# Sixteen small moves inside the core against one store to memory and four loads back, with a new order of the whole kernel

## The chip, the cores and the metric

The kernel runs on 1 core of a Trainium2 chip. The metric is the device time of one execution in microseconds (us), as the median of the runs; before, three runs took 598.32 to 598.87 us, the median 598.42 us. The engines are PE (TensorE: matmul, with PEld for its weight loads), DVE (VectorE), ACT (ScalarE), POOL (GpSimd) and SP (SyncE, which here only issues transfers). SBUF is the core's working memory, PSUM the memory that PE writes, DRAM the memory outside the core.

## The reference

Eight batches of 512 tokens in 8 heads of 64, and 32 states in each head, attend to each other; then everything goes through one feed-forward layer:

```python
scores = scale * np.matmul(x, state.transpose(0, 1, 3, 2))      # tokens read the states
a = softmax(scores); xread = np.matmul(a, state)
scores2 = scale * np.matmul(state, x.transpose(0, 1, 3, 2))     # states read the tokens
a2 = softmax(scores2); sread = np.matmul(a2, x)
y = concatenate([xread, sread], axis=2)                         # (8, 8, 544, 64) -> 4352 rows of 512
h = y @ w_in                                                    # 512 -> 2048
out = (h * clip(h + 3, 0, 6) / 6) @ w_out                       # 2048 -> 512
```

The inputs are x (8, 8, 512, 64), state (8, 8, 32, 64), w_in (512, 2048) and w_out (2048, 512), all float32; the output is (4352, 512).

## The kernel before, in words

**Steps.** The feed-forward layer is cut into 144 steps: 16 for each of the 8 batches of tokens, and 16 for the rows of all states together at the end. A step has a first product (`first`, `first_grouped`, `first_states`; lines 1225 to 1419 and 1664) into one of two PSUM banks `ps_h`. ACT and DVE then make g = h * clip(h + 3, 0, 6) of it (lines 1413 and 1416 in batches 0 to 2, lines 1250, 1252 and 1261 in batches 3 to 7, where seven blocks take the place of eight), and split g into a high and a low half of fewer bits (lines 460 to 497). In many steps of the later batches the low half is finished by a transfer of POOL that accumulates (line 497, 128 x 896 elements or so). The second product (`second`, `second_grouped`) multiplies the halves with those of w_out and adds up in four banks `acc0` to `acc3`. Every product is three matmuls on halves (line 1178). The tokens' own reading of the states is folded into the weights: `wprime` (line 768) multiplies the states with w_in (matmuls of line 700), and the first product takes the softmax weights `aT` against that.

**The attention of batch b** is spread over earlier steps. The states come in through four small transfers on SP's queue (`load_state`, line 634) and DVE transposes them (`turn_state`, line 645). x comes in twice, once as it is (`load_x`, line 668, tile `xb`, four quarters) and once in blocks for a transposition by DVE (`load_turned`, line 686, sixteen transfers into tiles `raw`; `take_in`, line 846). PE makes the scores (line 700, in `scores_by_columns`). DVE and ACT make the two softmaxes; `states` (line 1006) writes the exponentials of the states' scores into tiles `tmp`, key `e2` (ACT, line 1041). Batch 0 has a way of its own at the start of the kernel: PE transposes x (line 857), ACT copies it (line 864), PE makes the scores (line 921), and DVE takes the maximum (line 934) and so on.

**Around the change.** `weights_moved(b)` (line 1088, batches 1 to 7) turns the exponentials of one batch, 128 x 1024 float32, so that PE can use them as weights. DVE transposes blocks of 32 x 32 (line 1096) from `e2` into a tile `raw`, key `blocks`. Then sixteen transfers on SP's queue (line 1103) move the quarters of the partitions across: quarter q of `blocks`, part c, goes to partitions of quarter c, part q, of another `raw` tile, key `e2T`. One transfer is 32 partitions by 256 elements, 32 KB, from SBUF to SBUF. The reader is `tokens_read(b)` (line 1117): 64 small matmuls (line 1134) of `e2T` with x, which ride with the scores of batch b + 1 in one task of PE (`riders`, lines 971 to 989); batch 7's stand alone (line 1155).

**Tiles and order.** `raw` has three places (five from batch 2 on) that weights, turned x, `blocks` and `e2T` use in turn. Each piece of work is told to a `Plan` (line 192) with its engine, an assumed cost, what it reads and writes. The order in which all of it is issued, on every engine and queue, is one long list of numbers, `ORDER` (line 68, 2986 numbers); the plan only checks that it keeps the dependencies, and finds places for the tiles. Each engine and SP's queue work in that order and wait at the first thing that isn't ready.

Of the kernel before, what the change touches and what calls it, by code (L numbers as in the profile page):

```python
# [68 lines left out]
1 0 5 2 3 4 24 79 92 426 27 34 28 6 30 36 37 11 31 35 29 38 32 43 44 33 39 45 49 40 46 47 41 50 56 25 48 51 42 26 52  # L69
61 57 53 80 58 74 62 130 54 63 77 55 59 81 64 60 75 82 65 68 14 95 76 66 78 67 93 87 71 69 94 72 107 70 88 96 108 90  # L70
109 89 12 97 73 114 154 7 91 110 13 429 102 111 132 19 115 103 113 112 105 104 116 127 8 427 117 126 85 106 83 120 131
161 171 9 144 84 118 133 121 10 15 134 145 119 138 128 16 137 86 135 129 136 122 153 17 166 123 100 18 151 169 101 152
167 124 139 168 150 170 98 125 188 146 99 430 147 195 20 205 183 148 206 21 196 157 207 149 189 193 158 22 194 190 155
217 23 186 156 178 184 191 187 212 223 164 210 192 222 159 214 431 224 185 225 165 162 160 228 218 174 219 271 141 229
163 215 238 220 204 237 142 221 209 143 235 230 213 239 428 216 245 172 140 211 175 259 247 173 236 262 260 234 263
176 261 233 240 179 290 177 181 241 180 254 246 231 182 281 232 264 272 208 505 276 201 291 244 202 274 338 243 203
288 273 322 287 275 286 242 250 295 279 251 282 289 248 283 298 277 249 296 284 280 297 252 278 285 308 292 255 253
506 299 257 256 307 293 258 265 294 332 267 309 316 337 335 304 333 305 268 317 300 306 266 336 315 269 334 226 301
323 310 339 302 270 311 324 318 314 303 358 312 340 352 368 359 367 319 325 353 364 341 369 365 354 326 313 507 360
327 363 342 361 375 508 403 362 320 343 366 404 321 373 344 405 412 374 370 197 355 399 345 400 328 417 371 346 347  # L80
504 348 372 376 424 349 408 420 402 422 421 411 418 423 394 350 329 425 330 351 401 413 410 395 419 409 509 396 495
331 406 414 397 432 415 398 514 416 437 441 407 513 440 446 356 227 462 433 448 377 465 443 466 439 517 469 379 464
434 392 496 438 198 468 497 199 463 435 383 457 467 498 511 499 470 471 384 357 436 458 389 512 459 478 381 510 479
390 476 460 387 629 477 378 461 445 481 472 525 518 473 487 380 482 486 385 516 488 388 474 489 382 631 475 535 447
483 515 386 501 484 393 536 502 391 485 634 444 500 537 442 503 519 572 635 454 630 452 449 538 542 590 450 579 540
453 573 480 549 539 451 575 543 455 577 576 541 456 632 578 200 551 558 520 636 580 568 521 530 633 570 775 522 552
638 574 544 640 591 550 545 569 644 546 592 523 637 524 547 639 548 563 493 606 526 494 527 587 607 594 564 595 571
608 586 650 565 490 609 589 593 491 553 581 566 612 531 661 528 642 627 567 619 596 532 588 616 582 667 626 597 643
690 669 621 641 583 622 666 670 614 584 668 776 777 662 677 613 585 610 663 685 678 625 533 778 684 534 623 664 700
598 492 529 665 618 779 645 628 708 780 620 707 624 683 679 615 682 599 680 617 709 701 749 681 695 784 611 717 702  # L90
655 705 703 783 706 710 656 600 657 716 559 704 740 805 658 601 711 715 659 741 806 660 714 560 742 748 554 807 602
745 555 796 561 743 556 562 781 603 712 557 713 604 746 754 771 797 605 747 646 772 812 799 744 773 798 801 795 647
802 765 651 800 782 652 671 794 803 774 787 766 804 767 770 788 792 722 768 789 817 723 691 785 769 718 692 719 825
696 693 720 672 823 694 697 673 724 793 790 725 827 674 721 791 698 832 818 699 675 834 828 819 676 826 820 829 824
838 835 821 830 930 822 857 831 733 833 759 727 858 877 839 732 836 837 726 750 867 731 760 887 751 863 859 728 888
786 860 883 730 865 755 884 729 861 653 869 862 648 756 752 900 761 649 878 762 912 654 879 889 885 866 880 868 763
870 882 931 764 910 917 846 881 808 841 906 809 923 753 864 901 925 913 908 918 902 922 757 813 924 919 758 886 814
911 909 1012 920 903 921 847 810 815 734 1005 927 1013 929 735 1004 1015 904 1011 1014 1006 905 848 1009 736 1010 1017
1016 972 842 962 914 849 851 843 1019 928 844 852 999 845 963 1018 895 1020 1008 1000 964 907 811 926 915 1007 1001
965 1041 890 853 1002 854 932 1003 916 966 1042 855 967 737 1043 850 1047 689 935 973 896 1059 840 891 933 946 975 892  # L100
1051 1039 970 936 1069 968 1070 1037 934 1049 937 1064 1071 1060 1048 893 1053 1040 938 894 1067 974 1066 1044 1038
971 1068 969 1065 1086 1057 1045 1076 1061 1046 947 939 1062 856 1052 1094 897 1063 816 1055 940 1058 1100 1050 1082
948 1099 738 1088 1056 949 739 1054 1102 1106 1077 1085 941 1103 898 1084 1072 1078 899 1104 1105 942 1089 1079 1107
1074 1080 1073 1081 1087 1202 1095 1075 1029 1101 1117 687 1115 1032 1096 1090 1119 686 956 1083 1121 1036 943 1097
1026 1092 1113 1028 1098 1132 1033 1091 1126 1108 1130 1034 1203 1116 1035 1118 1109 1120 1205 1133 1129 1093 1030
1128 1110 1134 944 1111 1023 1204 1112 1127 1024 1122 1144 1206 1114 688 1146 1123 1021 1142 957 1161 1124 950 871
1131 1157 1125 1164 1031 1148 1162 1025 1165 1135 1027 958 1158 1163 1140 1022 959 1143 945 1160 1153 1149 1155 1136
1154 1141 1255 993 1137 1166 1138 1256 1150 960 1151 1145 1257 1156 961 1182 1258 1152 1167 1139 1259 1193 1183 1168
1147 1195 1159 1169 1184 1190 1196 1189 1185 1291 1186 1191 1170 1292 1192 976 1178 1171 1194 1207 1293 1187 1172 1177
1180 1188 1173 1208 1181 1174 1200 1209 1175 1176 1197 1179 1210 1239 1199 1211 1296 1212 1260 1240 1213 991 872 1214  # L110
1247 981 994 1261 1250 1217 1241 978 1198 1219 995 987 1252 1294 1242 1248 1251 982 1262 996 1249 1243 983 1254 1253
1218 1297 1221 1244 985 1215 1216 986 1276 1263 990 1245 1295 1246 1285 977 1264 1220 1274 873 1289 984 1287 1277 1222
989 1269 1275 1283 988 1265 1319 980 874 1266 992 997 1333 1267 1331 979 1320 1271 875 1273 1201 1278 1286 876 1227
1279 1335 998 1280 1321 1281 1284 1290 1329 1322 1288 1336 1367 1282 1337 1327 1368 1347 1323 1383 1369 1324 951 1370
1298 1371 1325 1338 1326 1339 1332 1268 953 1312 1381 1334 1377 1300 1343 1379 1313 1299 1314 1301 1375 1270 1315 1330
1348 1302 1349 1328 1340 1272 1231 1345 1344 1233 1303 1372 1394 1223 1346 952 1407 1373 1304 1341 1235 1374 1318 1305
1376 1384 1380 1396 1397 1382 1408 1392 1385 1391 1393 1401 1378 1306 1386 1390 1399 1226 1342 1387 1395 1225 1409
1423 1388 1230 1316 1410 1400 1317 1228 1411 1433 1350 1398 1234 1437 1419 1224 1412 1442 1307 1355 1389 1424 1450
1229 1413 1422 1443 1420 1425 1421 1414 1236 1417 1444 1438 1456 1354 1576 1426 1356 1445 1418 1415 1579 1427 1232
1436 1402 1577 1432 1353 1434 1454 1580 1428 1238 1435 1446 1431 955 1429 1475 1361 1416 1447 1308 1462 1430 1439 1237  # L120
1448 1491 1440 1453 1513 1463 1471 1449 1359 1477 1360 1578 1357 1464 1469 1365 1457 1508 1465 1366 1309 1473 1362
1511 1485 954 1452 1512 1310 1487 1466 1474 1493 1352 1514 1478 1509 1489 1479 1488 1494 1510 1476 1486 1472 1467 1470
1480 1492 1451 1495 1455 1613 1363 1481 1502 1496 1482 1468 1506 1358 1504 1500 1614 1364 1497 1546 1616 1351 1483
1548 1615 1498 1484 1503 1501 1490 1617 1544 1565 1499 1550 1563 1507 1311 1559 1515 1403 1405 1404 1536 1406 1529
1459 1460 1551 1516 1547 1537 1458 1549 1517 1560 1530 1518 1535 1562 1552 1531 1532 1538 1545 1566 1519 1564 1553
1666 1567 1581 1539 1554 1669 1540 1570 1505 1561 1555 1582 1597 1541 1583 1556 1568 1635 1542 1557 1584 1543 1585
1591 1569 1558 1589 1605 1586 1609 1670 1595 1598 1606 1587 1612 1608 1441 1588 1610 1667 1571 1647 1649 1599 1611
1607 1636 1668 1645 1643 1600 1651 1601 1637 1602 1596 1592 1638 1593 1533 1603 1652 1594 1639 1590 1604 1658 1671
# [1792 lines left out]
```

## Time and profile before

| | |
|---|---|
| median of three runs | 598.42 us |
| the profiled execution, its own time | 598.21 us |
| its span, first to last instruction | 596.4 us |
| mean granted clock of PE | 0.999 |
| instructions in the profile | 13389 |
| PE busy | 589.0 us, 99% |
| DVE busy | 481.6 us, 81% |
| ACT busy | 389.3 us, 65% |
| transfers of line 1103 | 112 of 32 KB |

The profile shows one execution. Busy time is the share in which an engine had an instruction under way; PE's matmuls are pipelined, so that their records overlap. Issuing a transfer doesn't count as busy. The chain of waits is followed back from the last instruction, at each step to what released it.

### The profile page before, as it was taken

To read this page: it belongs to the slowest core of one execution; us is meant where nothing else is said; L and a number is where in the kernel's file an instruction comes from. 1 tells how busy PE (TensorE), PEld (TensorE's weight loads), DVE (VectorE), ACT (ScalarE), POOL (GpSimd) and SP (SyncE) were. 2 spreads that over 40 slices of the span, in tenths; PEclk is the share of its full clock that TensorE was granted. 3 is DMA by queue.
4 is the path that set the end of the run, shared out by engine and by line. 5 is a ranking of instruction groups with operands and counts; after the bars stand their busy time and mean duration, and the time that the engine had idled before them with its cause. 6 is when DMAs were issued, how large, how long until landed. Compare 5 with 4: busy or idle time off the path is not lost.

```text
span 596.4 us, 13389 instructions
## 1 busy us (share of the span) xinstructions
PE 589.0 (99%) x5331; PEld 452.9 (76%) x5331; DVE 481.6 (81%) x911; ACT 389.3 (65%) x637; POOL 89.8 (15%) x112
## 2 busy tenths in 40 slices
PE   8999999999999999999999999999999999999997
PEld 6577778778654445888788877887888888888875
DVE  5989896598877998889999988978889977885342
ACT  5889788885868876757474747555646656473432
POOL 2000000113344311311011111111111111001000
PEclk9999999999999999999999999999999999999999
DMA  8999224567898894597553776785343732323002
GB/s 298 334 281 259 68 90 144 100 151 129 114 114 111 165 145 61 84 197 107 94 114 45 129 125 91 117 144 88 73 58 72 129 71 34 67 32 67 2 1 71
DMA packets 101951, 68.24 MB, mean 114 GB/s; under 512 B 67712, under 2 KB 94976, under 8 KB 101504
## 3 DMA queue, kind: packets, MB, share of 16 engines
q0 software_dynamic: 14400, 21.37, 29.5%
q1 hardware_dynamic: 87200, 45.82, 28.3%
q8 instruction: 42, 0.69, 0.5%
q10 hardware_dynamic: 288, 0.20, 0.1%
q14 instruction: 21, 0.17, 0.1%
HBM read 33.41 MB, written 8.91 MB: 71 GB/s over the span
## 4 chain that ended last, share of the span: by engine, by line
PE 93%; DVE 2%; SPq 2%; issue 1%; ACT 1%; DMA 0%; DVEq 0%
PE acc L1178 54%; PE ps_h L1178 30%; PE both L700 5%; PE ps_h L1134 1%; SPq L1103 1%; PE acc L1449 1%; PE ps_h L1890 1%; PE ps_h L700 1%; DMA st_raw<-in_state_dram 0%; SPq L634 0%; PE both L921 0%; SPq L686 0%; DVE w_in L576 0%; ACT g_hi L494 0%; DVE ot L936 0%
## 5 line engine op out<-in xcount | busy, mean ns | idle before, releaser
L1178 PE MATMUL ps_h<-aT,wp 128*128 128x256 f16 (+2 forms) x1146 | 163.6, 291 | 0.0
L1178 PEld LDWEIGHTS <-g_hi 128*128 128x128 f16 x1344 | 130.7, 98 | 34.3 <-issue 2.6
L1178 PE MATMUL acc<-w,g_hi 128*128 128x256 f16 (+1 forms) x704 | 130.8, 297 | 0.0
L1178 PEld LDWEIGHTS <-wp 128*128 128x128 f16 x1056 | 102.6, 98 | 24.6 <-issue 2.8
L1178 PE MATMUL acc<-T,g_hi 128*128 128x256 f16 x640 | 101.4, 273 | 0.7 <-ACT g_hi L494 0.7
L1178 PE MATMUL acc<-w,g_lo 128*128 128x256 f16 (+1 forms) x352 | 84.0, 297 | 0.0
L1178 PEld LDWEIGHTS <-g_lo 128*128 128x128 f16 x672 | 64.9, 98 | 20.3 <-issue 3.8
L1250 ACT ACTIVATE G<-ps_h,three 128x512 f32<-128x512 f32 x54 | 41.9, 777 | 37.9 <-PE ps_h L1178 26.3
L1178 PE MATMUL acc<-T,g_lo 128*128 128x256 f16 x320 | 64.2, 273 | 0.0
L497 POOL DMA_DIRECT2D g_lo<-G x34 | 29.3, 862 | 165.2 <-DVE g_lo L495 82.7
L1261 DVE TENSOR_TENSOR G<-G 128x256 f32<-128x256 f32 (+1 forms) x108 | 52.2, 486 | 1.7
L1178 PE MATMUL acc<-w_out_hi,g_hi 128*128 128x512 f32 x124 | 50.4, 406 | 0.0
L1178 PE MATMUL acc<-w_out_hi,g_lo 128*128 128x512 f32 x124 | 48.4, 390 | 0.0
L1178 PE MATMUL acc<-w_out_lo,g_hi 128*128 128x512 f32 x124 | 48.3, 390 | 0.0
L1413 ACT ACTIVATE g<-ps_h,three 128x512 f32<-128x512 f32 x48 | 34.3, 717 | 16.5 <-PE ps_h L1178 12.3
L1252 DVE SCALAR_TENSOR_TENSOR G<-G,ps_h 128x512 f32<-128x512 f32 x54 | 36.8, 682 | 6.7 <-ACT G L1250 6.6
L494 ACT CAST g_hi<-G 128x896 f16<-128x896 f32 x34 | 31.7, 934 | 14.6 <-DVE G L1261 9.8
L497 POOL DMA_DIRECT2D g_lo<-g x26 | 22.7, 873 | 122.2 <-DVE g_lo L495 72.6
L1416 DVE SCALAR_TENSOR_TENSOR g<-g,ps_h 128x512 f32<-128x512 f32 x48 | 32.5, 681 | 7.4 <-ACT g L1413 7.3
L468 DVE SCALAR_TENSOR_TENSOR g_lo<-G,g_hi 128x896 f16<-128x896 f32 (+1 forms) x31 | 26.3, 851 | 10.9 <-ACT g_hi L467 6.3
L1654 POOL DMA_DIRECT2D w_out_hi<-w_out_lo x16 | 17.4, 1196 | 116.9 <-PE acc L1178 113.9
L467 ACT ACTIVATE g_hi<-G 128x896 f16<-128x896 f32 (+1 forms) x31 | 23.4, 758 | 17.5 <-DVE G L1261 7.4
(200 smaller groups left out, 983.1 us busy)
## 6 DMA issues: line engine op xcount, KB each, us to landing
xb<-in_x_dram SPq DMA_DIRECT2D x32, 256.0 KB, 3.9
g_lo<-G POOLq DMA_DIRECT2D x34, 224.0 KB, 4.2
raw<-in_x_dram SPq DMA_DIRECT2D x112, 64.0 KB, 3.5
out_dram<-ot SPq DMA_DIRECT2D x10, 512.0 KB, 3.6
early<-in_moe_w_in_dram SPq DMA_DIRECT2D x5, 1023.0 KB, 6.6
w_out_hi<-w_out_lo POOLq DMA_DIRECT2D x16, 256.0 KB, 5.4
g_lo<-g POOLq DMA_DIRECT2D x18, 224.0 KB, 4.0
raw<-raw SPq DMA_DIRECT2D x112, 32.0 KB, 2.9
```

The source lines that it names most:

```text
L467: S(cost, rank, lambda: nc.scalar.mul(hi(), src(), by()), [*reads, *keys], first_, after)
L468: V_(cost, rank, lambda: nc.vector.scalar_tensor_tensor(lo(), src(), by(), hi() if hi().dtype == F16 else hi().bitcast(F32), op0=ALU.mult, ...
L494: S(cost, rank, lambda: nc.scalar.copy(hi(), src()), reads, [writes[0]], after)
L497: P__(0.87, rank, lambda: nc.gpsimd.dma_start(lo(), src(), accum_op=ALU.add), reads, [writes[1]], (), size)
L700: nc.tensor.matmul(out[q // 2 if by_pairs else u][at * NS : (at + 1) * NS, :], (made["stT", b] if left is None else left)[rows, cols], mov ...
L1178: nc.tensor.matmul(ps, l, r, start=start and k == 0, stop=stop and k == len(pairs) - 1)
L1250: S_(0.73, rank, lambda: nc.scalar.activation(g(), h(), AF.Relu, bias=three_of(G_SCALE / 4), scale=scales["gate7"]()), [ps, ("scale", "gat ...
L1252: V(0.63, rank, lambda: nc.vector.scalar_tensor_tensor(g(), g(), 6.0 * G_SCALE / 4, h(), op0=ALU.min, op1=ALU.mult), [ps], [key])
L1261: V(cost, rank, lambda out=out, one=one, other=other, op=op: nc.vector.tensor_tensor(blocks(*out), blocks(*one), blocks(*other), op=op), [ ...
L1413: S_(cost + (0.12 if scaled else 0.05), rank, lambda: nc.scalar.activation(g(), bank(ps)[:, :width], AF.Relu, bias=three_of(by), scale=sca ...
L1416: V(cost, rank, lambda: nc.vector.scalar_tensor_tensor(g(), g(), 6.0 * by, bank(ps)[:, :width], op0=ALU.min, op1=ALU.mult), [ps], [g_key])
L1654: X("P", 0.87, rank, lambda w=w: nc.gpsimd.dma_start(w("hi"), w("lo"), accum_op=ALU.add), [lo_key], [hi_key], after, 1.35)
```

## The change

In `weights_moved` the sixteen moves go. In their place the whole of `blocks` is stored to a tile in DRAM (`turned{b}`, 128 x 4 x 256 float32, 512 KB) in one transfer. Four transfers, one for each quarter c of the destination's partitions, read their 128 KB back from it into `e2T`. All five are on SP's queue; the four read what the first wrote, so that they wait for its landing. `ORDER` is replaced as a whole: it has 2909 numbers, 77 fewer (7 batches x 11), and nearly all other work has other places in it. No other line changes.

```diff
@@ ORDER
-1 0 5 2 3 4 24 79 92 426 27 34 28 6 30 36 37 11 31 35 29 38 32 43 44 33 39 45 49 40 46 47 41 50 56 25 48 51 42 26 52
...
@@ weights_moved
           [e2_key(b, g) for g in range(NG)], [(*blocks_key, g) for g in range(NG)])
+        there = dram.tile([P, P // NS, NG * P], F32, name=f"turned{b}")
+        plan.add("Q", 0.65, rank, lambda: nc.sync.dma_start(there, made_of(blocks_key).rearrange("p g s -> p (g s)").rearrange(
+            "p (k f) -> p k f", k=P // NS)), [(*blocks_key, g) for g in range(NG)], [("turned", b)], after, 500.0)
         for c in range(P // NS):
-            for q in range(NQ):
-                def move(c=c, q=q):
-                    nc.sync.dma_start(
-                        runs(e2T_key(b, 0))[quarter(c), q].rearrange("p m n -> p (m n)"),
-                        runs(blocks_key)[quarter(q), c].rearrange("p m n -> p (m n)"))
-                Q(rank, 35.0, move, [(*blocks_key, g) for g in range(NG)], [e2T_key(b, 0, c, q)], cost=0.65)
+            def move(c=c):
+                nc.sync.dma_start(
+                    runs(e2T_key(b, 0))[quarter(c)].rearrange("p q m n -> p q (m n)"),
+                    there[:, c].rearrange("(q p) f -> p q f", p=NS))
+            Q(rank, 140.0, move, [("turned", b)], [e2T_key(b, 0, c, q) for q in range(NQ)], cost=0.65)
```

What the new list does at the places that the prediction speaks of, read off the two lists:

- Start, x of batch 0 on SP's queue: quarters 0, 1, 2, 3 before; 3, 0, 1, 2 after. PE's first two score products of quarter 0 change places.
- State of batch 7: its load stands among the moves of batch 6 before; after, ahead of the store of batch 6.
- Batch 3's transfers, from the store on: store, one return, a turned x transfer, the 1024 KB store of batch 2's output, a turned x transfer, the three other returns. Before: sixteen moves, then that output's store.
- Of PE's 1133 tasks 138 keep their rank; the others shift by up to 27 ranks. In PE's list 84 pairs of neighbours stay neighbours.

## Rows read from the trace of the kernel before

**Rows 1.** Page, part 1: busy time, share of the span, instructions of each engine.
```profile
PE 589.0 (99%) x5331; PEld 452.9 (76%) x5331; DVE 481.6 (81%) x911; ACT 389.3 (65%) x637; POOL 89.8 (15%) x112
```

**Rows 2.** Busy time by stretch: PE, PEld, DVE, ACT, POOL; PE's clock, DMA share, GB/s.
```profile
0.00:25.00 25.00, 22.80 (x194) 16.07 (x195) 18.71 (x47) 16.50 (x34) 3.02 (x12) 1.00 0.90 312
25.00:100.00 75.00, 75.00 (x485) 56.00 (x484) 67.40 (x108) 63.34 (x123) 0.00 (x0) 1.00 0.63 180
...
400.00:410.00 10.00, 9.29 (x102) 7.66 (x101) 7.76 (x16) 6.42 (x10) 1.13 (x2) 1.00 0.68 114
...
500.00:592.00 92.00, 91.97 (x850) 77.49 (x847) 54.23 (x123) 40.57 (x67) 5.16 (x6) 1.00 0.19 36
592.00:596.40 4.40, 0.00 (x0) 0.00 (x0) 0.48 (x1) 0.15 (x1) 0.00 (x0) 0.87 0.42 119
```

**Rows 3.** Chain of waits, whole run: shares by line, and one piece (start, us, what).
```profile
PE acc L1178 54%; PE ps_h L1178 30%; PE both L700 5%; PE ps_h L1134 1%; SPq L1103 1%; PE acc L1449 1%; PE ps_h L1890 1%; PE ps_h L700 1%; DMA st_raw<-in_state_dram 0%; SPq L634 0%; PE both L921 0%; SPq L686 0%; DVE w_in L576 0%; ACT g_hi L494 0%; DVE ot L936 0%
...
530.08 3.06 PE acc L1178 x28
```

**Rows 4.** Chain of waits from 396 to 406 us: start, us, what.
```profile
395.87 0.59 SPq L1103
...
397.19 0.62 SPq L634
...
399.55 2.96 DMA st_raw<-in_state_dram
...
402.63 0.31 DVE stT L645
...
403.88 0.95 ACT g_hi L494
```

**Rows 5.** Line 1103, whole run: issue time in ns (min/median/max), and time to landing.
```profile
L1103 SPq DMA_DIRECT2D raw<-raw x112: 507/592/1514, 93.8 to 484.8; - x112
...
DMA to landing us min/median/max: 1.8/2.9/6.3
```

**Rows 6.** Page, part 6: transfers, KB of each, median us to landing.
```profile
raw<-in_x_dram SPq DMA_DIRECT2D x112, 64.0 KB, 3.5
out_dram<-ot SPq DMA_DIRECT2D x10, 512.0 KB, 3.6
```

**Rows 7.** Line 1501, the three stores of 1024 KB: time to landing.
```profile
DMA to landing us min/median/max: 4.2/6.5/8.3
```

**Rows 8.** Batch 3: SP's timeline, line 1103's landings from 250 to 262 us, PE's timeline.
```profile
247.72 6.60 SPq L1103 DMA_DIRECT2D raw<-raw  x8
...
DMA to landing us min/median/max: 2.7/4.1/6.3
...
260.13 1.20 PE L1134 MATMUL ps_h<-xb,raw 128*32 128x64 f32 x64
```

**Rows 9.** Tile xb, the first load alone, then the first two: time to landing.
```profile
DMA to landing us min/median/max: 3.1/3.1/3.1
...
DMA to landing us min/median/max: 3.1/3.3/3.4
```

**Rows 10.** Timeline of the start: start, us, engine, line, operation.
```profile
4.28 0.83 PE L857 MATMUL acc<-ident,xb 128*128 128x128 f32 x4
...
5.85 1.10 PE L921 MATMUL both<-sread_t,w_in 128*128 128x64 f32 x8
...
6.99 0.42 DVE L934 TENSOR_REDUCE m<-both 128x8 f32<-128x256 f32 x1 [1.46 <-PE both L921]
```

**Rows 11.** Groups by line and shape, batch 2's steps: busy us, mean ns of one | idle before.
```profile
L1413 ACT ACTIVATE g<-ps_h,three 128x512 f32<-128x512 f32 x48 | 34.3, 717 | 16.5 <-PE ps_h L1178 12.3 <-DVE nm L1037 2.3 <-DMA g_lo<-g 1.3
...
L1416 DVE SCALAR_TENSOR_TENSOR g<-g,ps_h 128x512 f32<-128x512 f32 x48 | 32.5, 681 | 7.4 <-ACT g L1413 7.3
...
L494 ACT CAST g_hi<-g 128x512 f16<-128x512 f32 x8 | 4.9, 612 | 0.6 <-DVE g L1416 0.6
```

236 rows, old and new, of the table ORDER are left out of this document.

## The prediction

> **What bounds the kernel now.** I read the page first. PE is busy 589.0 of 596.4 us, PEld 76%, every other engine less [rows 1]. A busy PE need not be a PE at its peak, so I asked for busy time by stretch [rows 2]: from 25 to 592 us PE has next to no idle time (75.00 of 75.00, 91.97 of 92.00 and the like in the stretches left out) except in one place, 400 to 410 us, where it is busy 9.29 of 10.00. It idles 2.20 us in the first 25 us and 4.40 us after its last matmul. What a full stretch hides shows in the chain of waits [rows 3]: 28 matmuls in 3.06 us are 109 ns each for 256 columns, which at the granted clock of 1.00 (the 2.4 GHz level) is 107 ns of columns. So from 25 us on PE is the bound, its instructions are the same before and after, and the change can only touch three things: the 0.71 us hole, the first 25 us (a chain, much of it fill-in matmuls), and new holes.
>
> The Trainium skill speaks against such a reading: by Perfetto Trace Analysis, section Identifying the Most-Contended Engine, matmul busy time does not tell how near the limit PE is, and LDWEIGHTS busy time should be used; at 76% that leaves room for 24%. The 109 ns per matmul decide here for the first reading; what the rule would give is rival D.
>
> The chain also spends 1% of the span, some 6 us, on SP's queue at line 1103, the sixteen moves [rows 3]. Most of that lies behind a full PE. The one place where it doesn't is the hole [rows 4]: SP still issues moves at 395.87, so the state load (line 634) goes out only from 397.19, its last part lands at 399.55 + 2.96 = 402.51, DVE stands in order before line 645 until then, its next sums come late, ACT's cast at 403.88 too, and PE waits 0.71 us for it.
>
> **The change part by part.** *Removed:* 7 x 16 = 112 issues on SP, 592 ns in the median [rows 5]: 66 us of SP. *Added:* 7 stores and 28 returns, 35 issues, 21 us at the same price, and a wait: the returns read what the store wrote, so SP stands until the store has landed. A 512 KB transfer from SBUF to memory lands in 3.6 us [rows 6]; that is 3.0 us of standing, 21 us for seven when nothing lies between. In the new order the first return follows its store at once for batches 2 to 4, and one to three other transfers lie between in the others. Behind the standing SP queue x loads, turned x loads and a state load. Even so SP is relieved by 24 us.
>
> *One batch's way:* before, 15 x 0.59 + 2.9 = 11.8 us from the first issue to the last landing if nothing is put between [rows 5]. After: store 3.6, three more issues 1.8, and a return's landing. No row has 128 KB from memory in runs of 1 KB; the 64 KB loads of x take 3.5 [rows 6], the fastest move 1.8, the slowest 6.3 [rows 5]. I take 3.5 (the same direction): 8.9 us. Bounds: 1.8 + 1.8 + 1.8 = 5.4 (the store as fast as the fastest move) and 8.3 + 1.8 + 6.3 = 16.4 (as slow as the slowest 1024 KB store [rows 7]). Per batch that is 3 us earlier, or 4 to 5 later at worst. On the path it is worth nothing while the reader, the 64 small matmuls of line 1134, stands further off. It is nearest in batch 3: the last move goes out at about 253.7 (end of the row 247.72 + 6.60, less one issue), its landing is the 6.3 of that stretch, 260.0, and the reader starts at 260.13 [rows 8]. Counting PE's work in the two order lists, the last return of batch 3 stands 4.0 us ahead of its reader, where the last move stood 6.3 us. A landing of 3.5 fits with 0.5 us to spare: price 0; bounds 0 and 6.3 - 4.0 = 2.3 us.
>
> *The hole at 404:* in the new order the load of state 7 stands ahead of store 6 and of all its returns, and 28 us of PE's work ahead of DVE's transposition of it, where it stood 4.4 us ahead. The transposition no longer waits: -0.71 us. Late next is the same cast behind DVE's sums, which have their inputs in SBUF by then. Bounds -0.71 and 0.
>
> *The start:* the new order issues x quarter 3 first, then 0, 1, 2. Quarter 0 landed 3.1 us after its issue at 0.74, at 3.9; the second issue, at 1.25, landed after 3.4, at 4.6 [rows 9]. So quarter 0 comes 0.7 us later, quarter 1 at the time of the old third. PE took quarter 0 at 4.28 and the scores from 5.85 to about 6.95, DVE's maximum began at 6.99 [rows 10]; DVE's and ACT's softmax then run nearly without a pause up to the main stream. New: quarter 0 at about 4.7, quarter 1 about 5.6 to 6.2, scores 6.25 to 7.35, maximum at 7.4. The lists also swap the two score halves so that the half that ACT copies first is used first; with quarter 1's transposes in front of them that gives nothing more. I take +0.40; bounds 0 (the loads overlap better) and +0.73 (all of the landing's delay).
>
> *Everything else that the new order moves:* PE keeps 84 of its neighbouring pairs of tasks, so nearly each product has another place. Most keep their distance to what feeds them. The exceptions lie in batch 2: the products of step 34 come 3.3 us of PE's work after its first product (before 6.3), those of step 32 4.1 (10.1), 37 4.8 (6.3), 41 4.8 (10.2). A step of batch 2 needs ACT 717, DVE 681 and ACT 612 ns [rows 11], 2.0 us and three hand-overs. They fit if neither engine is busy with something else; DVE is busy 81% of the run and ACT 65% [rows 1]. New holes: at least 0, at most three of the size of the one that there is (2.1). I take 0.35, half of one: the old order has just one in 567 us.
>
> POOL's accumulating transfers keep their order but for neighbours, 67 of 103 unmoved: 0. The stores and returns share the DMA engines with them; DMA is busy 63% from 25 to 100 us and 68% around 404 us [rows 2], and PE comes 9.9 us or more after the product that such a transfer finishes (11.1 in the old list): 0, at worst the 2.3 us above.
>
> **Sum** against the profiled execution, 598.21 us (span 596.4 and 1.8 around it): -0.71 + 0.40 + 0 + 0.35 = +0.04, so 598.25. It ran 0.2 us under the median of the three runs, 598.42; I forecast **598.3 us**, no change.
>
> **Rivals.**
> *A. The returns of batch 3 come late (slower).* For: the 0.1 us between last landing and reader before [rows 8], and 2.3 us less room in the list; in the new order a 1024 KB store stands among the returns, and such stores took up to 8.3 us. Against: that store is nearly 10 us of PE's work ahead of the last returns, and there are three late transfers instead of sixteen. It decides once a return takes over 4.0 us to land. At 6.3 PE stands 2.3 us at line 1134: 598.3 + 2.3 = 600.6. Chance 0.11.
>
> *B. ACT or DVE is busy when a shortened step comes (slower).* For: the four distances above. One instruction in the way is a hole of about the old size; three of them beyond the 0.35 make 2.1 - 0.35 = 1.75, so 600.0. Against: 3.3 us for 2.0 us of work. Chance 0.14.
>
> *C. The start is no later, or earlier (faster).* If PE's fill-in and the swapped halves take up the late quarter and return as much as the swap is worth, half the scores' 1.10 us, the start gives -0.55 instead of +0.40 and no new hole comes: 598.42 (the median) - 0.71 - 0.55 = 597.2, or a little below. Against: the later landing is on the first link of the chain. Chance 0.11.
>
> *D. The moves on the chain are the bound (faster).* PE has room that its busy time hides, and SP's 1% of the chain [rows 3] comes back whole: 598.4 - 6.0 = 592.4. Against: the full stretches [rows 2] and the 109 ns. Chance 0.03. (This is how it would go by the rule of the Trainium skill named above.)
>
> *E. SP is not relieved:* the waits for the stores cost what the issues saved, and the state load is late again. Then the hole stays, 598.3 + 0.71 = 599.0; still no change. Chance 0.06.
>
> **The numbers.** About 0.2% (1.2 us) is what this kernel's measurement can tell from no change. Forecast 0.55, E 0.06: within 0.2% 0.61. Slower (A, B) 0.25; faster (C, D) 0.14. The forecast's own range goes from no delay at the start and no new hole, 597.5, to the whole delay and one whole hole, 599.0. For eight in ten I add most of C below (597.0) and A and B up to 600.5; D and the far end of A are left out.
>
> **What would show it.** Right: line 1103 gone, 7 stores landing in about 3.6 us and 28 returns in about 3.5; PE full between 400 and 410; DVE's maximum at about 7.4 us; line 1134 of batch 3 without a wait. Wrong: PE idle before line 1134 near 260 (A), before products of steps 32 to 41 between 160 and 215 us (B), the first maximum at or before 7.0 (C), or busy stretches that are full while the span shrinks by several us (D).

## The result, and the profile after

The changed kernel took 603.76 us (median of ten runs, 600.97 to 608.14) where the kernel before took 599.25 us on the same chips (ten runs, 598.21 to 602.35). The ratio is **1.0067, 95% interval 1.0039 to 1.0095**: slower by 0.7%, some 4 us, where no change was forecast. The profiled execution took 603.62 us, 5.4 more than that of before.

The page's part 1, then the shares of its chain of waits (they answer to [rows 1] and [rows 3]):

```profile
PE 589.9 (98%) x5330; PEld 452.3 (75%) x5330; DVE 479.1 (80%) x911; ACT 390.2 (65%) x637; POOL 90.1 (15%) x112
...
PE 86%; DMA 5%; DVE 4%; issue 1%; ACT 1%; SPq 1%; DVEq 0%; ACTq 0%; POOLq 0%
PE acc L1177 50%; PE ps_h L1177 29%; PE both L697 4%; DMA g_lo<-G 2%; DMA g_lo<-g 1%; PE ps_h L1133 1%; SPq L683 1%; DMA xb<-in_x_dram 1%; DMA T<-raw 1%; PE acc L1448 1%; DMA raw<-in_x_dram 1%; DVE wp L465 1%; DVE w_in L573 0%; PE ps_h L697 0%; DVE ot L1325 0%
```

PE is as busy as before, and the moves are gone from the chain. In their place stand transfers that the change didn't touch: `g_lo`, which POOL's accumulating transfers finish, and `raw` and `xb`, the loads of x. (Line numbers are three lower than before ahead of the changed lines, one lower behind them: the product is line 1177 now.)

Busy time by stretch, with the columns of [rows 2]:

```profile
0.00:25.00 25.00, 22.24 (x189) 15.18 (x190) 17.94 (x44) 15.65 (x32) 3.03 (x12) 1.00 0.86 298
...
100.00:200.00 100.00, 99.52 (x655) 65.45 (x654) 75.16 (x171) 79.13 (x146) 31.74 (x36) 1.00 0.77 129
200.00:300.00 100.00, 99.11 (x982) 67.45 (x984) 88.78 (x152) 65.54 (x94) 19.12 (x22) 1.00 0.73 131
300.00:400.00 100.00, 98.06 (x1053) 83.33 (x1042) 87.67 (x160) 59.38 (x85) 14.68 (x17) 1.00 0.64 117
400.00:410.00 10.00, 10.00 (x110) 8.35 (x108) 8.27 (x15) 6.77 (x10) 2.59 (x3) 1.00 0.58 93
```

The hole at 404 us is filled: 10.00 of 10.00 where [rows 2] has 9.29. But the first 25 us lost 0.56 us more than before, and between 100 and 400 us, where PE had been full, 0.48, 0.89 and 1.94 us are missing. What PE waited for, over the whole run (us in total, times, longest):

```profile
PE acc L1177 <- DMA g_lo<-G: 1.7, 2, 0.9
PE both L697 <- ACT tmp L1038: 0.8, 1, 0.8
...
PE acc L697 <- DVE wp L470: 0.6, 1, 0.6
PE acc L918 <- ACT w_in L861: 0.6, 1, 0.6
PE ps_h L1177 <- DVE wp L465: 0.3, 1, 0.3
PE acc L1177 <- DMA g_lo<-g: 0.3, 1, 0.3
PE ps_h L1177 <- DVE g L1415: 0.2, 1, 0.2
```

The same view of the kernel before, its second and third line:

```profile
PE acc L1178 <- ACT g_hi L494: 0.7, 1, 0.7
PE acc L700 <- DVE wp L473: 0.7, 1, 0.7
```

The first of these is the hole at 404 us, which is gone; the second is still there, at 0.6 (line 470 now). The new waits for `g_lo` stand at 292, 398 and 382 us, that for `tmp` at 306, that for `w_in` in the first 25 us, those for `wp` of line 465 and for `g` at 190 and 180. Another 1.4 us of this execution lie after PE's last matmul, which ended 5.9 us before the end of the span (before 4.4); in the second profile of the changed kernel, below, that was 4.3 again. PE's busy time is 0.8 us more, which wasn't traced. Together: 0.56 + 3.3 (between 100 and 400 us) + 1.4 + 0.8, less the 0.71 of the hole, are the 5.4 us.

The new transfers themselves (part 6 of the page: KB each, median us to landing):

```profile
turned<-raw SPq DMA_DIRECT2D x7, 512.0 KB, 3.6
raw<-turned SPq DMA_DIRECT2D x28, 128.0 KB, 4.1
```

Their reader in batch 3 follows the scores without a pause: line 697 runs from 260.61 for 1.09 us, line 1133 from 261.63 for 1.10.

### The profile page after: what moved, and what is told of

It reads as the page before. It is cut to its first block, busy times and chain, and to the rows that moved or that the text cites. A ratio compares the mean times of both kernels' runs of the same rounds, so it can differ in the third digit from the quotient of the medians.

```text
span 601.8 us, 13282 instructions
## 1 busy us (share of the span) xinstructions
PE 589.9 (98%) x5330; PEld 452.3 (75%) x5330; DVE 479.1 (80%) x911; ACT 390.2 (65%) x637; POOL 90.1 (15%) x112
## 4 chain that ended last, share of the span: by engine, by line
PE 86%; DMA 5%; DVE 4%; issue 1%; ACT 1%; SPq 1%; DVEq 0%; ACTq 0%; POOLq 0%
PE acc L1177 50%; PE ps_h L1177 29%; PE both L697 4%; DMA g_lo<-G 2%; DMA g_lo<-g 1%; PE ps_h L1133 1%; SPq L683 1%; DMA xb<-in_x_dram 1%; DMA T<-raw 1%; PE acc L1448 1%; DMA raw<-in_x_dram 1%; DVE wp L465 1%; DVE w_in L573 0%; PE ps_h L697 0%; DVE ot L1325 0%
## 5 line engine op out<-in xcount | busy, mean ns | idle before, releaser
L1177 PE MATMUL acc<-T,g_hi 128*128 128x256 f16 x640 | 100.1, 273 | 0.0
L1653 POOL DMA_DIRECT2D w_out_hi<-w_out_lo x16 | 15.9, 1164 | 125.0 <-ACT g_hi L469 97.5
```

Of the source, the lines that this page charges most:

```text
L1177: nc.tensor.matmul(ps, l, r, start=start and k == 0, stop=stop and k == len(pairs) - 1)
L1653: X("P", 0.87, rank, lambda w=w: nc.gpsimd.dma_start(w("hi"), w("lo"), accum_op=ALU.add), [lo_key], [hi_key], after, 1.35)
```

## The experiments

All ratios below are to the kernel before, run on the same chips, with their 95% interval. Two theories stood: **O**, the new order costs the time; **T**, the new transfers cost it, by crowding the DMA engines.

### The new transfers alone

The old list of `ORDER`; of each batch's sixteen numbers for moves the first becomes the store, the fourth, eighth, twelfth and sixteenth the returns. Run twice.

```diff
 ORDER (of the kernel before), one batch's moves in the order in which they stand
-move 1  ... move 4 ... move 8 ... move 12 ... move 16
+store   ... return ... return ... return  ... return
```

> The old order with the new transfers: the store stands where the first of a batch's sixteen moves stood, the four returns where the fourth, eighth, twelfth and sixteenth did. Theory O: within 0.2% of the kernel before, or up to 0.7 us faster if the state load of batch 7 is no longer late (the hole near 404 us). Theory T: most of the loss is here, 3 to 5 us slower than before, with PE waiting for accumulating transfers that land 2 us later than before.

> The old order with the new transfers once more, beside the next kernel: 0.9974 at the first measurement, so 0.996 to 0.9985.

Measured: 598.33 us, **0.9974 (0.9962 to 0.9986)**, and again 598.50 us, 0.9980 (0.9968 to 0.9993). The transfers alone are a small gain. So the new list costs the whole loss and that gain: 1.0067 against 0.9977, 0.9%, some 5.4 us. PE is full from 400 to 410 us (10.00 of 10.00). The times are closer together as well, 597.4 to 598.7 in the first twelve runs and 597.6 to 599.8 in the second, where the kernel before has 598.1 to 602.4.

### The late state load alone

The kernel before, with its moves; one number of `ORDER` (the load of batch 7's state) is put ahead of batch 6's first move. Run twice.

```diff
-2278 2273 ... 1979 2265 2271
+1979 2278 2273 ... 2265 2271
```

> The kernel before, with its sixteen old moves, only with the state load of batch 7 ahead of the moves of batch 6 on SP's queue. If the gain of the new transfers under the old order (0.9974) is the late state load alone, this gets the same: 0.9965 to 0.998, PE full from 400 to 410 us. If it is the relief of SP's queue in other places too, this gets less than half: 0.9988 or more.

> The kernel before with the state load of batch 7 ahead of batch 6's moves, once more: 0.9987 at the first measurement, which leaves open whether the late load is all that the new transfers gain. If it is all, the two kernels differ by under 0.05%; if the relief of SP's queue brings more, the new transfers are 0.1% or more ahead of it.

Measured: 598.51 us, 0.9987 (0.9972 to 1.0001), and beside the second run of the new transfers 0.9983 (0.9970 to 0.9995), 598.45 us against 598.50. PE, by stretch:

```profile
400.00:410.00 10.00, 10.00 (x110) 8.36 (x108) 8.60 (x17) 7.05 (x12) 1.52 (x2) 1.00 0.82 134
```

The first figure lies between the two expected, and its interval just reaches no change; the second stands side by side with the new transfers and is the same. One moved load, which closes the hole at 404 us, brings what the new transfers bring, as far as intervals of 0.12% to either side can tell. SP's relief shows elsewhere too, without a gain in time. DVE's waits for turned x (us in total, times, longest): in the kernel before from 110 to 125 us, then over the whole run with the state load ahead, and with the new transfers in the old order:

```profile
DVE tmp L846 <- DMA raw<-in_x_dram: 4.0, 1, 4.0
...
DVE tmp L846 <- DMA raw<-in_x_dram: 4.2, 2, 3.9
...
DVE tmp L843 <- DMA raw<-in_x_dram: 0.2, 1, 0.2
```

PE stands for none of these.

### The new order with the old moves

```diff
 ORDER (of the changed kernel)
-store b; return c, four times
+batches 1, 3: sixteen moves at the first return; 2, 5: at the third; 4, 6, 7: four at each return
```

> The new order with the sixteen old moves; because the new order leaves fewer places in raw than the old moves want, all sixteen stand together at the place of the first return in batches 1 and 3 and of the third in batches 2 and 5, and four at each return in batches 4, 6 and 7. Theory O: as slow as the changed kernel, 1.005 to 1.010, for the new order is the loss. Theory T (new transfers crowd the DMA engines): 1.000 to 1.002. If the changed kernel gains from its transfers as the old order did, it is some 0.2% slower than the changed one: 1.009.

The even form, four moves at each return in every batch, would have been the cleaner test; its list wants more places than its tiles have, so there is no time for it.

Measured: 619.11 us, **1.0336 (1.0311 to 1.0361)**, far worse than either theory had said. PE's longest waits, and DVE's longest from 100 to 130 us:

```profile
PE ps_h L1152 <- DVE wp L473: 4.4, 1, 4.4
PE acc L1178 <- ACT g_hi L472: 4.3, 1, 4.3
PE both L700 <- DVE wp L473: 3.3, 1, 3.3
...
DVE tmp L846 <- DMA raw<-in_x_dram: 10.2, 1, 10.2
```

SP's timeline in that stretch (start, us, engine, line, operation, how many):

```profile
99.54 11.95 SPq L1103 DMA_DIRECT2D raw<-raw  x16
112.95 11.05 SPq L686 DMA_DIRECT2D raw<-in_x_dram  x13
```

Sixteen moves hold SP for 12 us, the turned x stands behind them, DVE stands 10.2 us for it, and PE behind DVE. Since the new list leaves fewer places in `raw` than the old moves want, they had to stand bunched, which makes this harsher than the old kernel's spacing; as a test of O against T it is spoiled. It suggests that the new list has already spent the SP time that the new transfers freed; what the old moves would cost there if they were spaced, no run shows.

### Crowding, by a second store

```diff
-lambda: nc.sync.dma_start(there, blocks)
+lambda: (nc.sync.dma_start(there, blocks), nc.sync.dma_start(again, blocks))
```

(Shortened: `blocks` stands for the tile and its rearrangement, and the second tile `again` is made one line above.)

> The changed kernel with each batch's store issued twice, the second into a tile of DRAM that nobody reads: 3.67 MB more on the DMA engines at the places where the changed kernel's transfers stand, the order untouched. Theory T (crowding is a large part of the loss): PE's waits for accumulating transfers grow by as much again as they had, 2 us, and the ratio goes from 1.0067 to 1.010 or more. Theory O (order): within 0.1% of the changed kernel, 1.006 to 1.0077.

Measured: 604.60 us, 1.0082 (1.0060 to 1.0104). That is between the two expectations. By the middle of the interval one more store costs 0.15%, 0.9 us, but the interval overlaps the changed kernel's, so whether crowding has a part stays open. In the waits that theory T named it doesn't show (line numbers are five higher here):

```profile
PE acc L1182 <- DMA g_lo<-G: 1.9, 3, 1.2
...
PE acc L1182 <- DMA g_lo<-g: 0.2, 1, 0.2
```

That is 2.1 us against 2.0 in the changed kernel, where T had 2 us more. Nor does it show in the accumulating transfers as a whole: they landed after 3.0/4.1/6.5 us (min/median/max) in the kernel before, 3.0/3.9/6.5 in the changed one and 3.0/3.8/6.7 here.

### Step 60's negation put back

The wait at 292 us: step 60's low half. DVE negates its high half (line 492), POOL adds the rest by a transfer, PE reads it. The changed kernel's timeline, DVE, POOL and PE:

```profile
282.48 1.21 DVE L883 TENSOR_TENSOR tmp<-tmp,s 128x1024 f32<-128x1024 f32 x1
284.81 0.69 DVE L1251 SCALAR_TENSOR_TENSOR G<-G,ps_h 128x512 f32<-128x512 f32 x1 [1.12 <-ACT G L1249]
285.42 0.39 DVE L492 TENSOR_SCALAR g_lo<-g_hi 128x896 f16<-128x896 f16 x1
...
286.34 0.86 POOL L494 DMA_DIRECT2D g_lo<-G  x1 [3.23 <-DVE G L1260]
...
292.78 0.61 PE L1177 MATMUL acc<-T,g_lo 128*128 128x256 f16 x4 [0.89 <-DMA g_lo<-G]
```

The transfer landed after 6.4 us. The negation had its input at 282.45 (the end of ACT's cast). But the new list puts it behind step 61's gate sum (line 1251), which waits 1.12 us for ACT and through it for PE. In the old list it stood ahead of that sum. The same place in the timeline of the kernel with the old order and the new transfers:

```profile
281.41 0.35 DVE L492 TENSOR_SCALAR g_lo<-g_hi 128x896 f16<-128x896 f16 x1
...
283.41 0.67 DVE L1251 SCALAR_TENSOR_TENSOR G<-G,ps_h 128x512 f32<-128x512 f32 x1
...
282.06 0.86 POOL L494 DMA_DIRECT2D g_lo<-G  x1 [0.77 <-DVE g_lo L492]
```

And its accumulating transfers from 280 to 284 us, steps 59 and 60:

```profile
DMA to landing us min/median/max: 6.7/6.8/6.9
```

Here step 60's transfer takes longer, 6.9 us, and PE doesn't wait: it was issued in time. The edit of the changed kernel:

```diff
-1419 1433 1420 1404 1409 1322 1425 1421 1405
+1419 1433 1404 1405 1420 1409 1322 1425 1421
```

> The changed kernel, only with step 60's negation on DVE and its accumulating transfer put ahead of step 61's gate sum on DVE, as the old order had it. Theory O (the order put the negation behind an instruction that waits for PE): the negation starts at about 283.8 us in place of 285.42, the transfer goes out some 1.7 us earlier, PE's wait of 0.9 us near 291.6 goes, and the kernel is about 0.9 us faster than the changed one. Theory T (the transfer is late because the store, the returns and loads share the DMA engines): it lands some 6.4 us after its issue wherever that is; at a start 1.7 us earlier the hole then goes as well, but the landing stays over 6 us; under theory O alone it lands in about 4.2 us.

Measured: 602.08 us, 1.0042 (1.0026 to 1.0058). The timeline has what was expected of the place:

```profile
283.81 0.38 DVE L492 TENSOR_SCALAR g_lo<-g_hi 128x896 f16<-128x896 f16 x1
285.01 0.69 DVE L1251 SCALAR_TENSOR_TENSOR G<-G,ps_h 128x512 f32<-128x512 f32 x1 [0.82 <-ACT G L1249]
```

The transfer goes out at 284.49, 1.85 us earlier, and lands at 290.0; PE's wait is gone, while that at 398 us grew from 0.85 to 1.23. The 5.5 us to the landing are between the two figures expected. In the kernel before, the same transfer landed after 5.2 us; sent at 286.34 it would have been there at 291.5, ahead of 291.9, where PE began to wait. So an earlier issue or a quicker landing would have closed this hole: the order made the transfer late, and a slow landing made the lateness visible. How much of the slow landing is the new transfers' doing stays open. It isn't the same in every execution: in the profiles of the next edit and of the one of step 35's gate, which leave this place alone, PE waits 0.42 and 0.39 us here.

### The quarters of x put back

```diff
-1 4 5 0 2 3 24 79
+1 0 5 2 3 4 24 79
```

> The changed kernel, only with x quarters of batch 0 issued 0, 1, 2, 3 again on SP's queue. If the start costs what PE's extra idle time of the first 25 us shows (2.76 against 2.20 us), it is 0.5 to 0.7 us faster than the changed kernel, some 0.55% above the kernel before, and PE's scores begin at about 5.85 us again. If the start is set by the work behind the scores, nothing changes: 0.67% above before.

Measured: 601.84 us, 1.0037 (1.0020 to 1.0054). The timeline of the changed kernel's start:

```profile
6.27 0.66 PE L854 MATMUL acc<-ident,xb 128*128 128x128 f32 x4 [0.16 <-DMA xb<-in_x_dram]
6.76 1.00 PE L918 MATMUL both<-sread_t,w_in 128*128 128x64 f32 x8
7.80 0.42 DVE L931 TENSOR_REDUCE m<-both 128x8 f32<-128x256 f32 x1 [2.18 <-PE both L918]
```

And of this one:

```profile
5.83 1.00 PE L918 MATMUL both<-sread_t,w_in 128*128 128x64 f32 x8
6.87 0.42 DVE L931 TENSOR_REDUCE m<-both 128x8 f32<-128x256 f32 x1 [1.46 <-PE both L918]
```

The first maximum comes 0.93 us earlier, PE's busy time in the first 25 us rises from 22.24 to 22.85. The scores of quarter 0 stand on PE behind the transposes of quarter 1, and those wait for quarter 1's landing. The trace accounts for 0.6 to 0.9 us, the ratio for 0.3% (1.8 us), with an interval of a microsecond on either side.

The intervals of these two single edits, and of the next, overlap the changed kernel's own, and the three ratios together would give back more (0.8%) than all repairs below (0.6%). So their times alone don't prove them; what each does is read from its timeline.

### A late load, and the scatter of the times

The changed kernel ran once more:

> The changed kernel itself once more, beside its repaired form and the same runs of the kernel before: 1.0067 of the kernel before at the first measurement, so 1.005 to 1.009 here.

Measured: 602.41 us, 1.0067 (1.0041 to 1.0093). Its profile is of an execution of 605.78 us, the longest of its six, and differs from the first mainly in one place (a wait of 0.46 us for ACT at 483 us is the next). DVE's longest wait from 160 to 190 us:

```profile
DVE tmp L843 <- DMA raw<-in_x_dram: 6.9, 1, 6.9
```

PE's timeline there:

```profile
178.61 1.46 PE L1177 MATMUL ps_h<-aT,wp 128*128 128x512 f16 x6
182.69 2.72 PE L1177 MATMUL ps_h<-aT,wp 128*128 128x512 f16 x6 [2.63 <-DVE g L1415]
```

PE by stretch (length, busy us and instructions, granted clock, DMA share, GB/s):

```profile
179.60:182.70 3.10, 0.47 (x4) 1.00 0.06 17
182.70:184.00 1.30, 1.30 (x4) 0.50 0.23 30
184.00:186.00 2.00, 2.00 (x6) 0.50 1.00 120
186.00:188.00 2.00, 2.00 (x17) 0.97 1.14 157
```

DVE stands 6.9 us for the last load of batch 3's turned x (4.5 in the first profile). It is the last of eight that go out one by one, in the first profile from 169.0 on, after SP has stood since 163.2 (DVE's first transposition of that x ends at 169.0). It goes out at 174.4 and 174.5; it lands after 5.66 us here and after 3.61 there. Step 35's gate (line 1415) stands behind the transposition on DVE, and PE waits for the bank that it frees: 2.63 us here, 0.19 there. Then the wait costs once more: behind it the granted clock is 0.50, the 1.2 GHz level, and the next product takes 2.72 us for 1.46. PE's busy time is 591.45 us in this profile, 1.6 more than in the first.

The edit puts step 35's gate ahead of that transposition:

```diff
-866 729 909 864 856 842 888 844 741 786 886 857 742
+866 729 856 857 909 864 842 888 844 741 786 886 742
```

> The changed kernel, only with step 35's gate (line 1412 on ACT, line 1415 on DVE) ahead of DVE's second transposition of batch 3's turned x (line 843), for whose last load DVE stands 4.5 us in one profile of the changed kernel and 6.9 in the other. If PE's wait near 180 us (0.2 us and 2.6 us in these two, for a PSUM bank that step 35's gate frees) comes from that load, it goes, the median falls by 0.5 to 2.5 us (a ratio of 1.003 to 1.006 to the kernel before), and the times lie closer together than the changed kernel's 601.0 to 608.1. If the wait comes from something else that varies, the ratio stays at 1.0067 and the spread as well.

Measured: 601.92 us, 1.0041 (1.0026 to 1.0055); twelve runs from 601.05 to 604.59. In the timeline, that of the fastest of the twelve, the gate now runs at 176.55, ahead of the transposition, and PE's wait near 180 us is gone:

```profile
176.55 0.69 DVE L1415 SCALAR_TENSOR_TENSOR g<-g,ps_h 128x512 f32<-128x512 f32 x1 [3.06 <-ACT g L1412]
178.08 1.25 DVE L843 STREAM_TRANSPOSE tmp<-raw 128x1024 f32<-128x1024 f32 x1 [0.83 <-DMA xb<-in_x_dram]
```

The spread proves nothing for this place: the two single edits above leave it alone, and their twelve runs lie as close together (600.8 to 604.5 and 600.5 to 604.1).

### Five places repaired, and a sixth

```diff
-1 4 5 0 2 3 ... 1420 1404 ... 1405 ... 1455 1362 1492 1485 ... 1923 1946 ... 1988 2003 ... 1990 2025 1968 1982 2023 2027
+1 0 5 2 3 4 ... 1404 1405 1420 ... 1485 1455 1362 1492 ... 1946 1923 ... 2003 ... 2025 1968 1982 2023 2027 1988 1990
```

> The changed kernel with the x quarters of batch 0 issued 0, 1, 2, 3 again and four more edits of the order at the holes that its trace shows: step 60's negation and transfer ahead of step 61's gate sum; the maximum over the scores of batch 5 (line 1034) ahead of step 63's subtraction on DVE; on PE the first product with step 82's low half behind the first product of step 86, and two products with step 86's low half behind three with step 87's. Theory O (the loss is these places of the new order): start 0.6, holes 0.95, 0.8, 0.27 and 0.86 us, in all 3.5 us less than the changed kernel, a ratio of about 1.001 to the kernel before, and none of the five waits in its list. If the loss lies elsewhere, or each wait only moves to the next reader, at most half of it comes back: 1.004 or more.

> The repaired kernel with the same edit. If the new order's loss is those six places, this is as good as the new transfers in the old order: 0.997 to 0.999. If the new order loses in many small places besides: 1.000 or more, as the repaired one.

Measured: repaired 599.39 us, **1.0006 (0.9984 to 1.0028)**; with the sixth place 599.28 us, 1.0000 (0.9986 to 1.0015). Five edits of a few numbers each give back 0.6 of the 0.9% that the list costs. The waits for `g_lo` by transfer are gone from the repaired kernel's list, the wait for `tmp` has shrunk to 0.4. The sixth place added next to nothing, and the timeline of one execution, 601.39 us and so one of the two longest of its twelve, shows what can happen there (the releaser that it names for DVE is inferred):

```profile
179.75 1.25 DVE L843 STREAM_TRANSPOSE tmp<-raw 128x1024 f32<-128x1024 f32 x1 [2.40 <-DMA xb<-in_x_dram]
...
182.99 0.60 PE L1177 MATMUL acc<-w,g_hi 128*128 128x512 f16 x2 [1.62 <-ACT g_hi L464]
```

The load is still late, DVE still stands for it, and PE's wait has moved on to another input. To the old order with the new transfers 0.2 to 0.3% are left. In the repaired kernel's profile PE still lacks 1.2 us between 100 and 400 us, 0.2%, in waits that the old order doesn't have: 0.4 for `tmp`, 0.3 each for `wp` of line 465 and for `g`, 0.2 for a `g_lo` by DVE. No edit was made for these.

## Why the prediction was wrong, step by step

**The bound.** PE's columns were the bound, as read: taking the moves off under an otherwise unchanged order gave 598.3 us, where rival D had 592.4. The rule of the Trainium skill (Perfetto Trace Analysis, section Identifying the Most-Contended Engine), that matmul busy time doesn't tell how near its limit PE is and LDWEIGHTS busy time should be used, stood behind rival D; the measurement decides against it here.

**The hole at 404 us, -0.71.** Right in place and direction: 10.00 of 10.00. The two kernels that close the hole in the old order gained 0.13 to 0.26%, 0.8 to 1.6 us, which is more than the 0.71 of the profiled execution; where the rest comes from isn't shown.

**The returns of batch 3, 0.** Right. The store landed after 3.6 us in the median, as taken; the returns after 4.1 where 3.5 was taken. Batch 3's last went out at 257.0 and landed after at most 3.3 us, more than a microsecond ahead of its reader at 261.63. Their issue cost SP 0.43 us in the median where 0.59 was taken. Rival A didn't come.

**The start, +0.40 with bounds 0 and +0.73.** Direction right, size too small: the maximum came at 7.80 where 7.4 was said and [rows 10] has 6.99. The prediction knew that quarter 1's transposes stand in front of quarter 0's scores, and had PE at them from 5.6 to 6.2 us; PE had to wait for their load and began at 6.27. Rival C fell with this.

**"Everything else that the new order moves", +0.35 with bounds 0 and 2.1, and "POOL's accumulating transfers", 0.** These two steps failed. Both measured room in PE's list: so many us of PE's work from a step's first product to the second. That is room only if the engines between do the step's work at once. Step 60 has more of it in the new list than in the old, 16.2 us against 14.2, and PE still waited 0.89 us: DVE's list had another instruction in front, which itself waited, and the transfer then took 6.4 us to land. The prediction compared PE's, SP's and POOL's lists and not DVE's and ACT's, though DVE is busy 80% of the time and takes its instructions in their order (the negation stood ready from 282.45 to 285.42). It looked for short distances in batch 2 alone, before 215 us. The measured price of the new places in the first profile is 0.48 + 0.89 + 1.94 = 3.3 us, above the upper bound of 2.1, and 2.8 of it lie behind 200 us. That is one execution; the five repairs of such places and of the start gave 0.6% back, some 3.6 us.

**Rival B** was the nearest: slower, by DVE, with PE idle between 160 and 215 us. Its mechanism was a busy engine; what happened near 180 us is an engine that stands for a load. Its 1.75 us became 0.2 to 2.6 us of waiting there, and more where the clock fell; the larger part of the loss lies outside its stretch.

**Rival E** (SP not relieved) fell: the state load is no longer late, and in the old order DVE's longest wait for turned x goes from 4.0 to 0.2 us (0.4 in the second run). In the new list it is 4.5 us again, at a later place: the list spends part of the relief on later loads.

In one sentence: the transfers gain about 0.2%, as much as moving one state load ahead in the old list gives; the new list, needed for none of it, loses 0.9%, and five places in it account for 0.6 of that.

## What to carry to other kernels

A distance in the bound engine's list isn't slack: follow the step through every queue between, and see what is queued ahead of each of its instructions, above all one that itself waits. When a local edit comes with a new order of everything, run the edit in the old order and the old order with only the one thing repaired that the edit repairs; here either came out ahead of both kernels of this case, by 0.1 to 0.3% of the one before. At step 60 the slower landing, 6.9 us, cost nothing where the issue was early, and 6.4 us cost 0.9 where it was late. The Trainium skill's advice to issue a transfer early and wait for it late (DMA: Bandwidth & Descriptors, section Rules for kernel authors) agrees with this.

## What the runs showed of the hardware that was not expected

A wait of 2.63 us of PE was followed by the granted clock at 0.50, the 1.2 GHz level, from 182.7 to about 186 us, so that the product behind it took 2.72 us and PE's busy time grew by 1.6 us; behind the waits of 0.9 us at 292 us and 1.62 us at 183 us the clock stayed at 1.00. The same load of 64 KB took 3.6 us in one execution and 5.7 in another at the same place in the order. Both fit the scatter of the changed kernel's times, 601.0 to 608.1: its three longest executions of 16 (605.78, 607.09 and 608.14 us) are those with the lowest mean granted clock, 0.996 and 0.997, the others have 0.998 to 1.000. Only the first of the three has a profile, so the cause in the other two isn't shown.
